# Preparing weights beside the attention and parking them off the chip in a fused attention, gMLP and mixer kernel

## The chip, the cores and the metric

The kernel runs on one NeuronCore of one Trainium2 chip. The metric is the device time of one launch in microseconds, the median of three runs. The profile is of one execution, taken by the hardware profiler. TensorE is called PE, VectorE DVE, ScalarE ACT, GpSimd POOL; SP is the engine whose queue issues nearly all DMAs.

## The reference

```python
q_pool = q.reshape(4, 8, 576, 2, 64).mean(axis=3)
attn = softmax(q_pool @ k.T / 8)          # 576 x 1152 for each of 4*8 heads
x = heads_side_by_side(attn @ v)          # 4 x 576 x 512
h = gelu(x @ w_in)                        # w_in 512 x 1024
u, v = h[..., :512], h[..., 512:]
v_n = layernorm(v) * g_ln
v_s = einsum('ts,bsd->btd', w_sg, v_n) + b_sg[:, None]   # w_sg 576 x 576
x = x + (u * v_s) @ w_out                 # the gating block, w_out 512 x 512
x = x + (relu(x.T @ w_tok1) @ w_tok2).T   # token mixing, 576 -> 256 -> 576
out = x + relu(x @ w_ch1) @ w_ch2         # channel mixing, 512 -> 1536 -> 512
```

All inputs but `w_sg`, `g_ln`, `b_sg`, `q`, `k`, `v` arrive as float64 and have to be turned into float32 on the chip.

## The kernel before, in words

Every product but two of the attention's is made in three passes: a float32 is split in a high part (a float32r copy) and a low part (what the copy lost), and PE multiplies high by high, high by low and low by high (`products`, line 186). So each weight block has two tiles, high and low (`block`, line 179).

**A conversion** (`convert`, line 216) turns one 128 x 512 piece of a float64 weight into these two tiles. A DMA brings the 64-bit words into `ws` (512 KB, two buffers). ACT works out which numbers are in range (`wd`, lines 230 and 231). DVE builds the float32 in `wz` in four operations (lines 239, 243, 247 and 252). POOL copies it to the high tile (line 210) and subtracts to get the low one (line 214). `Feed` keeps a list of pieces: `add` appends and starts loads, `ops(1)` issues one of the four steps, and `until(n)` issues what is missing so that n pieces are done. The table `HOOKS` says at which points of the program a step is issued: "c" is one step of a conversion, "n" one of the layer norm, "x" one split of x, "t" and "s" the preparation of `w_sg`, "f" one of three closing steps of the attention. A name such as `2U1e` means batch 2, phase U, block 1, at its end; the trailing letter tells the place within the block.

**Attention** (`attention`, line 329) takes 16 pairs of heads. Each pair's work is handed to a planner (`Plan`, line 57) as tasks with an engine, an estimated duration, an urgency and the buffers that it takes and gives back; `Plan.run` lists them in the order in which a simulated machine would start them, and the instructions are issued in that order. Each engine runs its own instructions in that order. For one pair: q and k are loaded, POOL adds neighbouring rows of q (line 388), PE transposes q and k (lines 400 and 432), PE makes scores (line 462) and DVE their row maxima (line 469); then PE makes the scores turned round (line 513), ACT takes the exponential (line 521), POOL adds the exponentials up in `acc` (line 527), PE multiplies by v (line 536), PE sums `acc` over partitions (line 549), DVE inverts the sum (line 560) and writes x (line 567). Scores of both kinds share three PSUM buffers. Of the weights only the first block, the half of `w_in` that makes v (four pieces), is converted here, one step of the 16 about every 26 us. Its first two loads are issued by `feed.add` ahead of the plan, so ahead of q and k.

**Gating** (`spatial`, line 717), for each batch b: V (line 807) makes v for 576 tokens in groups of 256, 256 and 64, followed by gelu on ACT and DVE (lines 707 to 714) and statistics (lines 820 and 821); O (line 915) multiplies the batch before by `w_out`; U (line 873) makes u in four blocks with gelu; S (line 891) is the product with `w_sg`, after which DVE adds the bias (line 900), POOL multiplies by u (line 903) and ACT and DVE split the result (lines 905 and 906). The layer norm (`v_norm`, line 826) runs between, in small pieces; its low parts are POOL's (line 858, shown as line 214 of the helper). V, U and S of all batches share three PSUM buffers of two banks. In batch 0 the kernel also converts the u half of `w_in` (four pieces, loaded through ACT's queue and SP's) and `w_out` (four), and prepares the gate's matrix `w_sg`: it is loaded into `gu`, split by ACT and POOL (`wsg_split`), transposed by PE in both parts and copied out by ACT (`wsg_tr`, line 764). U's block fb waits until its piece is converted, and S waits for all of `w_sg`.

**Mixing** (`mixing`, line 1034): K (line 1088) and Q (line 1098) are the two token products, with transposes of x between (line 1070). Then nine chunks of 256 tokens each take a channel product (`psc`, line 1151), transposes (`pu`, line 1163) and a second channel product (`po`, line 1171). From batch 3's U on, 30 pieces are converted here: 12 of `w_ch1`, 6 of the token weights, and 12 of `w_ch2`, the last ones in the first chunk, between its products.

## Time and profile before

| | |
|---|---|
| median of 3 runs | 1238.43 us (1237.66 to 1239.03) |
| the profiled execution | 1238.36 us, of which the span from first to last instruction is 1236.5 us |
| busy PE, DVE, ACT, POOL | 94%, 58%, 37%, 49% of the span |
| mean granted clock of PE | 0.978 of full speed |

Full speed of PE's clock is 2.4 GHz and its other level 1.2 GHz, so a granted clock of 0.81 over a stretch is a mix of the two. A busy share says little by itself: PE shows 94% busy and still the time goes up and down with the stretches in which it isn't. The stages have to be read one by one: attention to about 564 us, gating from there to about 832 us, token mixing to 910 us, channel mixing to the end.

### The profile page before, as it was taken

Reading aid. Unit: us, or ns where it says so; the run is one execution under the profiler, and the core shown is the slowest. Engines: PE = TensorE matmul, PEld = TensorE weight load, DVE = VectorE, ACT = ScalarE, POOL = GpSimd, SP = SyncE. Lnnn points to the kernel's source line nnn. Section 1 sums busy time; section 2 is a strip of 40 time slices with the busy share of each in tenths; the row PEclk is TensorE's granted clock in tenths of the full one; section 3 lists DMA queues with packets and bytes.
Section 4 is the critical chain, followed back from the end, with each engine's and each line's share of the span. In section 5 each row is a group of like instructions: output and inputs, shape, how many; then the busy total and the mean of one; then the engine's idle time right before and its main releaser. Section 6 shows DMA issues by size and latency. Waiting matters only on the chain.

```text
span 1236.5 us, 22054 instructions
## 1 busy us (share of the span) xinstructions
PE 1162.6 (94%) x9269; PEld 949.0 (77%) x9269; DVE 711.1 (58%) x1017; ACT 458.5 (37%) x847; POOL 611.5 (49%) x452
## 2 busy tenths in 40 slices
PE   3899999999999999998579999979989999999998
PEld 2577777777767777765569898968877899999887
DVE  4767767776676666643976464799987112121111
ACT  1244454445444444453552423434433111111111
POOL 1477877877777777786473414263365111100100
PEclk9899999999999999998789999989998999999999
DMA  6412222222122211002220000023232000000000
GB/s 149 94 40 59 59 56 58 59 59 59 44 55 59 52 46 39 21 1 77 69 62 17 1 1 1 18 69 111 88 100 86 10 17 10 17 18 18 18 17 18
DMA packets 63332, 57.32 MB, mean 46 GB/s; under 512 B 39936, under 2 KB 51968, under 8 KB 63232
## 3 DMA queue, kind: packets, MB, share of 16 engines
q1 hardware_dynamic: 62176, 54.85, 16.3%
q8 instruction: 73, 1.20, 0.4%
q10 hardware_dynamic: 1056, 1.05, 0.3%
q14 instruction: 27, 0.22, 0.1%
HBM read 51.17 MB, written 4.72 MB: 45 GB/s over the span
## 4 chain that ended last, share of the span: by engine, by line
PE 37%; DVE 10%; ACT 1%; issue 1%; POOL 1%; DVEq 0%; ACTq 0%; POOLq 0%
PE psc L1151 11%; PE po L1171 11%; PE pss L891 5%; PE psv L807 3%; DVE wz L247 2%; PE psu L873 2%; PE psz L915 2%; DVE wz L243 2%; DVE wz L252 1%; DVE wz L239 1%; DVE y L214 1%; PE pso L915 1%; PE pu L1163 1%; DVE xT L1102 1%; PE psh L1098 0%
## 5 line engine op out<-in xcount | busy, mean ns | idle before, releaser
L527 POOL TENSOR_TENSOR acc<-acc,e 128x576 f32<-128x576 f32 x224 | 319.7, 1427 | 83.6 <-ACT e L521 65.2
L469 DVE TENSOR_REDUCE mx<-s 128x2 f32<-128x768 f32 (+1 forms) x240 | 225.8, 950 | 115.1 <-PE s L462 111.9
L521 ACT ACTIVATE e<-sT 128x576 f32<-128x576 f32 x288 | 184.2, 652 | 180.0 <-PE sT L513 172.9
L462 PE MATMUL s<-k,q 64*128 64x384 f32 (+1 forms) x1440 | 178.7, 351 | 2.5 <-DVE mx L469 1.9
L513 PE MATMUL sT<-q,k 64*128 64x288 f32 x1728 | 177.3, 307 | 2.6 <-DVE mx L469 1.9
L513 PEld LDWEIGHTS sT<-q,k 64*128 64x128 f32 x1728 | 135.4, 185 | 44.3 <-issue 34.5
L536 PE MATMUL po<-e,vn 128*64 128x288 f32 x1152 | 160.1, 413 | 0.0
L1151 PEld LDWEIGHTS psc<-x,w 128*128 128x128 f32 x1296 | 156.8, 190 | 3.3 <-DVE gc L1078 2.5
L1151 PE MATMUL psc<-x,w 128*128 128x256 f32 x1296 | 157.1, 283 | 2.3 <-DVE gc L1078 2.3
L1171 PE MATMUL po<-w,gc 128*128 128x512 f32 x648 | 156.4, 401 | 2.3 <-POOL w L214 1.7
L1171 PEld LDWEIGHTS po<-w,gc 128*128 128x128 f32 x648 | 121.8, 189 | 32.9 <-POOL w L214 2.5
L462 PEld LDWEIGHTS s<-k,q 64*128 64x128 f32 (+1 forms) x1440 | 116.3, 178 | 19.0 <-issue 10.3
L1077 ACT ACTIVATE gc<-psc 128x256 fp32r<-128x256 f32 x108 | 41.0, 384 | 229.9 <-PE psc L1151 229.9
L536 PEld LDWEIGHTS po<-e,vn 128*64 128x64 f32 x1152 | 75.3, 136 | 60.8 <-issue 20.1
L1078 DVE SCALAR_TENSOR_TENSOR gc<-psc,gc 128x256 fp32r<-128x256 f32 x108 | 45.5, 424 | 100.2 <-ACT gc L1077 100.2
L210 POOL TENSOR_SCALAR x<-xT 128x1024 fp32r<-128x1024 f32 x9 | 9.6, 1069 | 173.6 <-PE psc L1151 173.2
L1178 DVE TENSOR_TENSOR ob<-po,us 128x512 f32<-128x512 f32 x18 | 12.4, 691 | 133.5 <-PE po L1171 133.5
L513 PE MATMUL sT<-nmT,pick 64*128 64x288 f32 x576 | 88.2, 290 | 0.0
L560 DVE RECIPROCAL den<-den 128x288 f32<-128x288 f32 x32 | 62.3, 1947 | 35.6 <-ACT den L556 35.6
L891 PE MATMUL pss<-wsg,vn 128*128 128x288 f32 x448 | 74.6, 315 | 1.8 <-POOL vn L214 1.8
L891 PEld LDWEIGHTS pss<-wsg,vn 128*128 128x128 f32 x448 | 63.9, 193 | 12.0 <-issue 5.4
L873 PE MATMUL psu<-x,w 128*128 128x288 f32 x384 | 56.0, 307 | 10.1 <-issue 8.6
(117 smaller groups left out, 1519.0 us busy)
## 6 DMA issues: line engine op xcount, KB each, us to landing
ws<-in_moe_w_ch_dram SPq DMA_DIRECT2D x24, 512.0 KB, 3.5
qn<-in_q_dram SPq DMA_DIRECT2D x32, 288.0 KB, 4.4
kn<-in_k_dram SPq DMA_DIRECT2D x32, 288.0 KB, 4.1
vn<-in_v_dram SPq DMA_DIRECT2D x32, 288.0 KB, 3.2
out_dram<-ob SPq DMA_DIRECT2D x18, 256.0 KB, 2.0
ws<-in_moe_w_in_dram SPq DMA_DIRECT2D x6, 512.0 KB, 4.7
ws<-in_moe_w_out_dram SPq DMA_DIRECT2D x4, 512.0 KB, 3.5
gu<-in_moe_w_sg_dram SPq DMA_DIRECT2D x1, 1152.0 KB, 5.8
```

The lines of the kernel that those rows point to most:

```text
L462: nc.tensor.matmul(ps[0:m, h, 0:KC], flat(c.q[x])[r, t * P:t * P + m], c.k[y][r, cs], start=(n == 0), stop=(n == 2))
L469: nc.vector.tensor_reduce(out=mx[i % 2][0:m, t, :, g], in_=ps[0:m, :, 0:KC], axis=AX.X, op=ALU.max, negate=True)
L513: nc.tensor.matmul(ps[:, h, 0:TC], left, right, start=(n == 0), stop=(n == 3))
L521: nc.scalar.activation(out=s.e[j], in_=ps[:, :, 0:TC], func=AF.Exp)
L527: eng.tensor_tensor(out=s.acc, in0=s.e[0] if j == 1 else s.acc, in1=s.e[j], op=ALU.add)
L536: nc.tensor.matmul(s.po[D * h:D * h + D, 0:TC], c.vn[:, h, j], s.e[j][:, h], start=(j == 0), stop=(j == J - 1))
L560: nc.vector.reciprocal(out=s.den, in_=s.den)
L873: nc.tensor.matmul(ps[:, ch, 0:TC], wiu[sw][:, cc, fb * P:(fb + 1) * P], X[sx][:, cc, ch * TC:(ch + 1) * TC], start=first, stop=end)
L891: nc.tensor.matmul(ps[:, ch, 0:TC], V[sx][r, ti, db * P:(db + 1) * P], L.ws[sw][r, ti, ch * TC:(ch + 1) * TC], start=first, stop=end)
L1078: nc.vector.scalar_tensor_tensor(out=l_, in0=ps, scalar=0.0, in1=f32(h_), op0=ALU.max, op1=ALU.subtract)
L1151: nc.tensor.matmul(ps, WC1[f // 4][sw][:, cc, (f % 4) * P:(f % 4 + 1) * P], u[sx][:, cc], start=first, stop=end)
L1171: nc.tensor.matmul(pos[tt], g[sx][:, f, tt * P:(tt + 1) * P], WC2[f // 4][sw][:, f % 4], start=(f == 0 and n == 0), stop=(f == NF - 1 and ...
```

## The change

- Conversions become objects (`Piece`) with a destination tile or one off the chip. The high part is now a copy by ACT; before it was a copy by POOL.
- Within the attention the planner now also places the four pieces of the v half of `w_in`, the four of the u half, the preparation of `w_sg` (five row blocks; transposed in float32 by PE, then split by ACT and DVE) and the four of `w_out`, one about every 25 us from 60 us of the plan's time. All but the first four are stored in DRAM by SP's queue from the place of their own source buffer, and fetched back at the start of the gating.
- No load of a weight goes ahead of the first loads of q and k: each waits for a marked score task.
- The twelve pieces of `w_ch2` are converted in batches 1 and 2 of the gating, one step in the middle and one at the end of each block, stored in DRAM, and fetched when mixing starts. The steps in the channel products' first chunk are gone. The pieces of `w_ch1` and of the token weights stay where they were.
- The last third of the last product with v, the last sums and x's last half pair are kept out of the plan and issued among batch 0's V products. Batch 0's splits of x go from POOL to DVE.
- The bias loads and POOL's scaling of them move from the end of batch 0's U to just after V's second group of products.
- The planner looks at 300 tasks, before at 90; the two loads of a pair's q, k or v are one task.

```diff
+    def halves(x):
+        x = x.bitcast(F32R)
+        return [x[:, s * 512:(s + 1) * 512] for s in range(2)]
...
+        def high(self):
+            if self.dst:
+                self.parts = self.dst()
+                for x in self.parts[2:]:
+                    g_scale(x, self.z, 1.0)
+            else:
+                self.parts = [self.cut(x) for x in halves(self.s)]
+            nc.scalar.copy(self.parts[0], self.z)
+        def low_part(self):
+            sub(nc.gpsimd, self.parts[1], self.z, f32(self.parts[0]))
+        def send(self, s):
+            nc.sync.dma_start(out=self.away[s], in_=f32(self.parts[s]))
...
+    def fetch(to, x):
+        for s in range(2):
+            nc.sync.dma_start(out=f32(to[s]), in_=x[s])
...
-        for n in range(4 * CC):
-            plan.add("DVE", 0.75, lambda: feed.ops(1), urgency=20.0 + 26.0 * n)
-        feed.add(*row_block(0, w_in[:, DH:2 * DH], 0))
+        def conversion(x, u):
+            a = plan.add("SP", 0.05, lambda: x.load(nc.sync), after=[mark(u)], urgency=u - 20,
+                         take=["ws"], land=4.0)
+            d1 = plan.add("DVE", 1.2, x.step1, after=[a], urgency=u, take=["wz"])
+            e = plan.add("ACT", 1.4, x.early, after=[a], urgency=u, take=["wd"])
+            d2 = plan.add("DVE", 1.3, x.step2, after=[d1], urgency=u + 0.5)
+            d3 = plan.add("DVE", 1.3, x.step3, after=[d2], urgency=u + 1)
+            d4 = plan.add("DVE", 1.3, x.step4, after=[d3, e], urgency=u + 1.5,
+                          give=[("wd", e)] + ([] if x.away else [("ws", a)]))
+            h = plan.add("ACT", 0.65, x.high, after=[d4], urgency=u + 2)
+            l_ = plan.add("POOL", 1.4, x.low_part, after=[h], urgency=u + 2, give=[("wz", d1)])
+            if x.away:
+                for s in range(2):
+                    plan.add("SP", 0.05, lambda s=s: x.send(s), after=[h, l_][s:s + 1],
+                             urgency=u + 3 + s, land=3.5, give=[("ws", a)])
...
+        todo = [w0_piece(j) for j in range(CC)] + col_pieces(A.w1, w_in, 0)
+        todo += list(range(NTT)) + col_pieces(A.wo, w_out, 0)
+        for n, x in enumerate(todo):
+            u = 60.0 + 25.0 * n
+            if isinstance(x, int):
+                gate_weights(x, u)
+            else:
+                conversion(x, u)
+        for n in range(3):
+            feed.add(*row_pieces(A.c2[n], w_ch2, 512 * n))
...
         def finish():
-            yield lambda: None
-            yield lambda: None
+            yield lambda: [f() for f in rest[:-2]]
+            yield lambda: [f() for f in rest[-2:]]
             yield lambda: a2.close()
...
+            if name[0] in "12" and name[-1] in "mz":
+                feed.ops(1)
...
         def open_up(close):
             close()
             open_left()
-            splits.extend([lambda ti=ti: wsg_split(ti) for ti in range(CC)])
-            pieces.extend([lambda ti=ti, s=s: piece(ti, s) for ti in (CC, *range(CC))
-                           for s in range(2 if ti < CC else 1)])
-            L.io = feed.add(*col_block(2, w_out, 0))
+            for s in range(2):
+                nc.sync.dma_start(out=f32(L.ws[s][:, 0:CC]), in_=A.ws[s][:, 0:CC])
+                for r in range(0, P, TAIL):
+                    nc.sync.dma_start(
+                        out=f32(L.ws[s][r:r + TAIL, CC:NTT]), in_=A.ws[s][0:TAIL, CC:NTT])
+            fetch(L.wo, A.wo)
+            bias_load()
...
-        wsg_load()
+        fetch(W[1], A.w1)
...
+        fetch(W[4], A.c2[0])
...
-            feed.add(*row_block(i, w_ch2, 512 * (i - 4)))
+            fetch(W[i], A.c2[i - 4])
...
-                    feed.until(io + f + 1)
-                    hook(f"N{f}")
```

In the new `HOOKS` batch 0 has "f" after V's first products (`0V0a`), at the end of V's first group (`0V0z`) and after V's second products (`0V1a`); "x" for x's splits at `0V0m` (two), `0V1m`, `0V2a` and `0V2e`; and no "c". The "c" entries from batch 3's U to `Q31` and `M10` are as before.

## Rows read from the trace of the kernel before

**Rows 1.** Busy time by stretch: attention, batch 0, batches 1 and 2, then S3 to Q3.
```profile
core 0: us, PE busy (x) PEld busy (x) DVE busy (x) ACT busy (x) POOL busy (x), PEclk, DMA share, GB/s
52.00:564.00 512.00, 509.35 (x5186) 370.10 (x5184) 341.72 (x435) 249.82 (x455) 396.98 (x271) 1.00 0.19 47
564.00:653.00 89.00, 62.40 (x338) 52.56 (x335) 64.06 (x85) 41.97 (x82) 55.15 (x46) 0.81 0.25 78
...
653.00:764.00 111.00, 111.00 (x712) 101.35 (x710) 58.57 (x103) 36.33 (x56) 39.90 (x33) 1.00 0.00 1
...
801.00:911.00 110.00, 99.04 (x602) 85.31 (x601) 104.80 (x140) 46.56 (x76) 52.49 (x48) 0.97 0.29 89
```

**Rows 2.** PE in order of time, 563 to 633 us: start, duration, instruction, [idle before].
```profile
563.25 3.13 PE L536 MATMUL po<-e,vn 128*64 128x288 f32 x24
571.05 1.23 PE L549 MATMUL pt<-acc,ones 128*64 128x288 f32 x4 [4.67 <-POOL acc L527]
...
598.77 5.30 PE L873 MATMUL psu<-x,w 128*128 128x288 f32 x24 [8.59 <-issue]
...
633.01 19.92 PE L891 MATMUL pss<-wsg,vn 128*128 128x288 f32 x112
```

**Rows 3.** PE in order of time, 902 to 953 us.
```profile
904.58 6.01 PE L1098 MATMUL psh<-x,r 128*128 128x288 f32 x43 [0.99 <-DVE r L1078]
910.42 8.71 PE L1151 MATMUL psc<-x,w 128*128 128x256 f32 x72
...
953.10 17.99 PE L1151 MATMUL psc<-x,w 128*128 128x256 f32 x144
```

**Rows 4.** SP's queue at the start, and PE's first work.
```profile
0.73 0.86 SPq L221 DMA_DIRECT2D ws<-in_moe_w_in_dram  x2
...
5.35 0.60 SPq L379 DMA_DIRECT2D kn<-in_k_dram  x1
...
15.48 1.09 PE L432 MATMUL pt<-ident,kn 128*128 128x128 f32 x4 [15.48 <-DMA kn<-in_k_dram]
```

**Rows 5.** Attention: transposes among PE's other work; DVE, POOL and PE around 93 us.
```profile
365.33 0.66 PE L432 MATMUL pt<-ident,kn 128*128 128x128 f32 x4
...
92.74 3.15 DVE L243 SCALAR_TENSOR_TENSOR wz<-ws,wz 128x512 int32<-128x512 int32 x1
...
92.68 2.65 POOL L388 TENSOR_TENSOR qs<-qn 64x1152 f32<-64x1152 f32 x1 [1.17 <-PE pt L400]
...
96.81 0.67 PE L513 MATMUL sT<-q,k 64*128 64x288 f32 x6 [0.99 <-DVE mx L469]
```

**Rows 6.** What writes `wz`, 60 to 560 us (3 pieces): busy DVE and POOL.
```profile
60.00:560.00 500.00, 15.53 (x12) 5.71 (x6) 1.00 0.19 47
```

**Rows 7.** The chain that ended last, batch 2: V, U and S without a stall.
```profile
707.57 13.99 PE psv L807 x60
...
734.27 12.72 PE psu L873 x96
746.99 17.93 PE pss L891 x112
```

**Rows 8.** DVE and ACT behind batch 0's first V group, in order of time.
```profile
572.86 1.95 DVE L560 RECIPROCAL den<-den 128x288 f32<-128x288 f32 x1 [7.42 <-ACT den L556]
574.85 1.65 DVE L567 TENSOR_TENSOR xT<-os,den 128x288 f32<-128x288 f32 x1
582.88 1.22 DVE L708 SCALAR_TENSOR_TENSOR sq<-sq,psv 128x1024 f32<-128x1024 f32 x1 [6.38 <-ACT sq L707]
...
586.77 0.69 DVE L820 BATCH_NORM_STATS2 lst<-gv 128x6 f32<-128x512 f32 x1
...
584.35 1.06 ACT L713 ACTIVATE sq<-sq 128x1024 f32<-128x1024 f32 x1 [1.51 <-DVE sq L708]
```

**Rows 9.** POOL before batch 0's S: the low parts of the layer norm.
```profile
628.82 4.63 POOL L214 TENSOR_TENSOR vn<-gv,vn 128x512 fp32r<-128x512 f32 x3 [1.78 <-ACT vn L857]
```

**Rows 10.** The page's DMA issues: KB each, us to landing.
```profile
gu<-in_moe_w_sg_dram SPq DMA_DIRECT2D x1, 1152.0 KB, 5.8
```

**Rows 11.** What writes `wz`, 801 to 953 us (28.75 pieces): busy DVE and POOL.
```profile
801.00:953.00 152.00, 99.23 (x115) 59.07 (x59) 0.96 0.29 89
```

**Rows 12.** POOL between S3's last two gate products.
```profile
824.05 0.98 POOL L210 TENSOR_SCALAR x<-wz 128x512 fp32r<-128x512 f32 x1 [1.50 <-DVE wz L252]
```

**Rows 13.** The chain that ended last: two later channel chunks.
```profile
988.77 17.20 PE psc L1151 x144
1005.96 0.87 PE pu L1163 x8
1006.84 16.80 PE po L1171 x72
```

More of the change, by code (lines that the diff above doesn't have):

```diff
@@ L67, in ring, with add @@
         self.rings[name] = (n, [])
-    def add(self, eng, dur, fn=None, after=(), urgency=0.0, take=(), give=(), land=0.0):
+    def add(self, eng, dur, fn=None, after=(), urgency=0.0, take=(), give=(), land=0.0,
+            late=False):
         t = dict(eng=eng, dur=dur, fn=fn, after=[x for x in after if x], urgency=urgency,
-                 take=list(take), last=[], land=land, end=None, n=len(self.tasks))
+                 take=list(take), last=[], land=land, late=late, end=None, n=len(self.tasks))
         for ring, owner in give:
@@ L182, with far @@
     W = [block(wvp, "w0")]
+    away = ctx.enter_context(tc.tile_pool(name="away", bufs=1, space=bass.MemoryType.DRAM))
+    def far(name, shape):
+        return [away.tile(shape, F32, name=f"{name}{s}") for s in range(2)]
     PASSES = ((0, 0), (0, 1), (1, 0))
@@ new lines, with __init__, cut, load @@
+    class Piece:
+        def __init__(self, src, dst=None, away=None):
+            self.src, self.dst, self.away = src, dst, away
+            self.r, self.a, self.n = src.shape
+        def cut(self, x):
+            return x[:self.r, 0:self.a * self.n].rearrange("p (a n) -> p a n", a=self.a)
+        def load(self, eng):
+            s = cvp.tile([P, 512], I64, tag="ws", name="ws")
+            eng.dma_start(out=self.cut(s), in_=self.src)
+            self.s = s
+            w = s.bitcast(I32).rearrange("p (c t) -> p c t", t=2)
+            self.top, self.low = (self.cut(w[:, :, j]) for j in (1, 0))
+        def early(self):
+            self.d = d = self.cut(cvp.tile([P, 512], F16, tag="wd", name="wd", bufs=1))
+            nc.scalar.activation(out=d, in_=self.top, func=AF.Abs, scale=2.0 ** -20)
+            nc.scalar.activation(out=d, in_=d, func=AF.Abs, bias=m1024[:self.r])
+        def step1(self):
+            self.z = self.cut(cvp.tile([P, 512], F32, tag="wz", name="wz"))
@@ L276, in load, with steps @@
             while self.todo and len(self.ready) + (self.live is not None) < 2:
-                self.ready.append(convert(*self.todo.pop(0)))
-        def early(self):
-            self.cur[0]()
+                self.ready.append(self.todo.pop(0))
+                self.ready[-1].load(nc.sync)
+        def steps(self, x):
+            x.step1()
+            x.early()
+            yield
+            x.step2()
+            yield
+            x.step3()
+            yield
+            x.step4()
+            x.high()
+            x.low_part()
+            if x.away:
+                for s in range(2):
+                    x.send(s)
         def ops(self, n):
@@ L661, in tasks @@
                 po = None
+                last = i == NPAIR - 1 and x == 1
                 for js in ((0, 1, 2), (3, 4, 5), (6, 7, 8)):
@@ L666, in tasks @@
                                   take=["po"] if po is None else [],
+                                  late=last and js[-1] == J - 1,
                                   give=[("e", es[j]) for j in js] +
@@ L679, in tasks @@
-                r_ = plan.add("DVE", 2.0, lambda x=x: over(i, x), after=[d_], urgency=at + 8)
+                              urgency=at, take=["den"], give=[("tr", s_)], late=last)
+                r_ = plan.add("DVE", 2.0, lambda x=x: over(i, x), after=[d_], urgency=at + 8,
+                              late=last)
                 plan.add("DVE", 0.5, lambda x=x: x_out(i, x), after=[r_, o_], urgency=at + 9,
-                         give=[("os", o_), ("den", d_)])
+                         give=[("os", o_), ("den", d_)], late=last)
@@ new lines, in attention @@
+        for n, x in enumerate(todo):
[6 more added lines that the diff above has]
+            feed.add(*row_pieces(A.c2[n], w_ch2, 512 * n))
+        early = []
+        rest = []
+        order = plan.run()
+        for n, t in enumerate(order):
+            if n == len(order) - 40:
+                for ti in range(len(EARLY_ON)):
+                    early.append(x_early(ti))
+            if t["late"]:
+                rest.append(t["fn"])
+            elif t["fn"]:
@@ L925, in wo_act @@
             yield
-        splits, pieces, lns, xs_ = [], [], [], []
+        lns, xs_ = [], []
         def hook(name):
@@ L1147, in mixing @@
             for f in range(NF):
[L1148 removed]
+                feed.until(count[f] if i == 0 else 0)
                 ps = pc1.tile([P, 512], F32, tag="c1", name="psc1")[:, 0:NB]
```

218 lines of the change are left out of this document (96 added, 122 removed), and 40 rows, old and new, of the table HOOKS.

## Prediction

> **What bounds the kernel now.** I read busy time by stretch first, then PE in order of time where PE is not full, then the chain that ended last. In the attention PE is busy 509.35 of 512 us, in batches 1 and 2 of the gating 111 of 111 [rows 1]: PE sets the pace there, and the other engines have room (DVE 342 of 512 and 59 of 111). Three places leave PE waiting. At the start it does nothing until 15.48 us, when k lands [rows 4]. In batch 0, 564 to 653 us, it is busy 62 of 89 us at a granted clock of 0.81 [rows 1]; a whole batch without a stall is V 13.99 + U 12.72 + S 17.93 = 44.6 us, O left out, since batch 0 has none [rows 7]. From 801 us DVE is busy 104.8 of 110 us with conversions [rows 1], and the first channel chunk takes 953.10 - 910.42 = 42.7 us where a later one takes 17.20 + 0.87 + 16.80 = 34.9 us [rows 3, 13]. The change works on all three and pays with work put where PE is full.
>
> **The start.** Before k's second half, eight DMAs are queued: 2 of 512 KB (`ws`), then six of 288 KB, kn's second being the issue at 5.35 us [rows 4]. That is 2752 KB, landed at 15.48 us. Now only four of 288 KB (qn, kn) come first. If time goes by bytes, 1152 of 2752 KB of the 14.75 us since the first issue gives 6.2 us, a gain of 8.6 us; if only the 1024 KB of `ws` are saved, it is 5.5 us. I take **-7** (ends -8.6 and -5.5), and it reaches the end because PE is full from 52 to 564 us.
>
> **The attention's added work.** PE gets 25 transposes for `w_sg`. Four transposes among other PE work take 0.66 us, four alone 1.09 us [rows 5, 4]: 4.1 to 6.8 us, nothing hides them. I take **+4**, since they stand among other work. DVE gets eight more conversions at 15.53/3 = 5.2 us [rows 6] and ten subtractions, about 48 us on 342 of 512; POOL and ACT get some 10 and 25 us on 397 and 250. This is hidden unless it makes a row maximum late. It can: at 92.74 us a step lasted 3.15 us beside a POOL addition from 92.68 to 95.33 us, and PE then waited 0.99 us for a row maximum [rows 5]. The three converted pieces in this stretch hold two such losses, 0.65 us each piece, so eight more pieces cost about 5 us; the planner now knows these steps and puts row maxima first, so I take **+4** (ends 0 and 10). SP's stores and loads stand in one queue with q, k and v: a late store delays a load, but each pair's loads are asked for most of a 32 us period ahead.
> The Trainium skill (SBUF — State Buffer, "Who interferes with whom") says that a DVE instruction with two SBUF inputs and a GpSimd instruction that reads SBUF exclude each other for a whole instruction. The 3.15 us agree with it. By it alone, nothing would be added to the sum, as long as DVE's idle third takes the waits; it feeds the slower rival below.
>
> **The handover and batch 0.** The last scores end about 563.3 us, and now 563.25 us starts only half of the 24 last products with v (3.13 us) [rows 2]; V's first group follows at 564.8. Its 24 products are 13.99/60 = 0.233 us each [rows 7]: to 570.4. Then the other half of the v products to 572.0, and the sums, whose `acc` is ready at 571.05 [rows 2], so the 4.67 us of waiting are gone: to 572.7. V's second group runs to 578.3. What is late next is **DVE**: the sum's copy and V's square on ACT to 574.3, then front 1.22, tanh 1.06, back about 1.22, statistics two times 0.69 with a small aggregate each, reciprocal 1.95, x's last pair (at most 1.65, the row beside a busy POOL), to about 582.5 [rows 8]; only then the split of the tail of x, to 583.2, so V's third group of 12 products ends at 586.0; the second group's gelu and statistics take DVE to 588.5, and x's first two splits and the third group's front, 0.7 us each, to 590.6. So U starts at 590.6, not 598.77 [rows 2]. U no longer waits for conversions: 12.72 us and about 1.3 for a lowered clock after two idle stretches of 5 us, to 604.6. Then the last gelu and the layer norm's last low parts on POOL, three for 4.63 us [rows 9]: S in effect starts at 610.2 and ends at 629, against 633.01 + 19.92 = 652.9 [rows 2]. That is **-24**.
> The fetched weights: `gu` brought 1152 KB in 5.8 us [rows 10]; at that pace the u block (2 MB) lands ten us after attention's end, before U. The second `w_sg` tile, `w_out` and the bias wait for memory that x's last pair frees at 582.5: 3.8 MB, an estimate of 19 us, to 602. POOL's scaling of the bias stands in POOL's queue ahead of all low parts, so it is the one new wait that counts; at 602 us it only just clears. Ends: PE alone, 564.8 + 14 + 2.3 + 12.7 + 17.9 = 612, so -41; with POOL free 10 us later, -14.
>
> **Batches 1 and 2.** 48 steps, 12 pieces, spread over 58 places. A piece costs DVE 99.23/28.75 = 3.5 us at the end of the kernel and 5.2 in the attention [rows 11, 6]: 42 us on 58.6 of 111, so 91% busy, with the 5.2 end 109%. In 801 to 911 us, at 95%, PE lost 10% of its time [rows 1], part of it by waits that have nothing to do with DVE. Two `ws` buffers now come back only after a store; store and next load are some 9 us of a cycle of 8 to 10, so a step may wait for its load with gelu queued behind it on DVE, and PE's three buffers are the cover. I take **+5** (ends 0 and 14).
>
> **Mixing.** S3 to K2 keep their conversions. The high part leaves POOL: its 0.98 us stand between the last two gate products [rows 12], so **-1** (ends -3 and +4, the latter for 2 MB of `w_ch2` fetched in front of the pieces' loads). From Q2 on no steps are left: the first chunk becomes like the later ones, 42.7 - 34.9 = 7.8, and the 0.99 us wait in Q3 goes [rows 3]: **-9** (ends -10 and -4). The other 4 MB have 24 us until the second channel product needs them.
>
> **The sum.** -7 + 4 + 4 - 24 + 5 - 1 - 9 = -28. Against the profiled execution, 1238.36 us (the median is 1238.43, the same), that is 1210.4, so 1210.
>
> **The rivals.** (a) The forecast, 1200 to 1220: chance 0.46. (b) DVE's chain in the handover is covered by PE's buffers, nothing in the attention or batches 1 and 2 is late: -41, 0 and 0 instead of -24, +4 and +5, so 1184, about 1190 with half of it: 0.19. For it speaks that PE was never held up long in the attention [rows 1]; against it the DVE chain counted above. (c) The way back from DRAM is late: POOL stands at the bias, low parts and S wait, -14 or worse, 1220 to 1226: 0.14. For it speaks the one SP queue with 5 MB; against it `gu`'s pace. (d) DVE becomes the bound of batches 1 and 2, +14 and more for slower gates, 1219 to 1228: 0.13. (e) **Slower**: conversions in the attention come as four steps in a row beside POOL's additions, each 3 us as at 92.74, and three score buffers are used up by the first of them. To pay for everything else (-32 without the disturbance) twelve pieces would have to hold PE 2.7 us each, four times the 0.65 us seen; at 4 us each it is +48 - 32, 1254. Chance 0.06: DVE idles a third of the attention, but in pieces. (f) The change doesn't do what it says: S still waits for the parked `w_sg` as long as for its preparation, and the mixing's gain is eaten in (d): about 1236, 0.02.
>
> **How the numbers follow.** Likeliest is (a), 1210. Leaving out half of (b), all of (e) and (f) and a little at each edge, the range is 1191 to 1228. A measurement of this kernel tells 0.2%, 2.5 us, from no change. Faster by more than that holds (a) to (d) and parts of the rest: 0.93; within it 0.02; slower 0.05.
>
> **What would show it.** PE's first transposes near 8 us; attention's end near 564, as the start's gain pays for the added work; V's first product without a gap behind the attention, U at about 590 and S's end near 629; DVE about 90% busy in batches 1 and 2 with PE idle 5 us; a first chunk of 35 us with no `wz` in it. I am wrong if row maxima hold PE for over 10 us in the attention, if POOL's scaling of the bias ends after 605, or if PE idles over 14 us in batches 1 and 2.

## The result, and the profile of the changed kernel

| | before | changed |
|---|---|---|
| device time, median | 1238.05 us | 1255.35 us (1254.34 to 1257.3) |
| ratio | | 1.0145, 95% [1.0125, 1.0166] |
| profiled execution: its time, its span | 1238.36, 1236.5 us | 1255.77, 1253.2 us |

The kernel became **slower by 17 us** where I had predicted 28 us less. I cut both traces at the same events on PE and set each difference beside the term of the sum that it answers to ("psc" is the first product of the channel mixing):

| stretch | before | changed | difference | predicted |
|---|---|---|---|---|
| span's start to first transpose of k | 15.48 | 8.67 | -6.8 | -7 |
| to the end of the last scores | 547.8 | 558.6 | +10.8 | +8 |
| to V of batch 1 | 89.5 | 68.7 | -20.8 | -24 |
| **V of batch 1 to V of batch 3** | 112.0 | 147.1 | **+35.1** | **+5** |
| **to the first psc** | 145.7 | 152.5 | **+6.8** | **-1** |
| the first chunk | 42.7 | 34.9 | -7.8 | -9 |
| the rest | 283.4 | 282.8 | -0.6 | 0 |

Four terms were near, two were not, and those two make the sign. The stretches of the changed kernel by busy time, columns as in [rows 1]: attention, handover and batch 0, batches 1 and 2, to the first psc, first chunk.

```profile
8.67:567.30 558.63, 541.24 (x5391) 392.44 (x5393) 429.64 (x521) 276.51 (x509) 421.66 (x278) 0.99 0.30 75
567.30:636.02 68.72, 56.52 (x296) 46.75 (x297) 36.01 (x57) 21.08 (x35) 24.65 (x20) 0.85 0.35 124
636.02:783.10 147.08, 121.97 (x718) 108.38 (x717) 93.61 (x148) 57.51 (x91) 54.41 (x43) 0.94 0.26 86
783.10:935.57 152.47, 137.86 (x835) 120.58 (x833) 113.30 (x170) 63.43 (x107) 44.77 (x34) 0.96 0.20 65
935.57:970.44 34.87, 34.87 (x227) 31.57 (x226) 6.29 (x14) 5.68 (x14) 6.90 (x4) 1.00 0.31 121
```

The third row is the case. PE was full there before [rows 1]; now it is busy 121.97 of 147.08 us. 25.1 us are idle, and another 10.0 are the same products at a lower granted clock (0.94 on the mean, a mix of the two levels). DVE, the engine that got the work, is busy 93.61 us: 64%, not the 91% I had worked out, and still PE waits. For whom, in that stretch (us in all, times, longest):

```profile
PE psz L1016 <- DVE gv L844: 7.2, 3, 3.5
PE psu L974 <- DVE xT L1025: 6.5, 6, 1.9
PE pss L992 <- POOL vn L216: 6.2, 2, 4.8
PE psu L974 <- DVE gu L844: 3.0, 2, 2.4
PE pss L992 <- DVE gu L844: 2.2, 2, 1.4
```

18.9 of the 25.1 us end on DVE (the last step of a gelu, `gv` and `gu`, and the residual `xT`), 6.2 on POOL's low parts of the layer norm.

**The handover** went by the prediction's steps in the main. PE in order of time:

```profile
574.49 1.68 PE L574 MATMUL po<-e,vn 128*64 128x288 f32 x12
...
...
587.38 1.20 PE L908 MATMUL psv<-w,x 128*128 128x512 f32 x4 [2.39 <-DVE x L216]
591.11 2.29 PE L974 MATMUL psu<-x,w 128*128 128x288 f32 x8 [2.52 <-ACT x L355]
...
616.15 20.04 PE L992 MATMUL pss<-wsg,vn 128*128 128x288 f32 x104 [1.83 <-POOL vn L216]
```

The other half of the v products stands between V's groups, and V's third group waits for DVE's split of x. That U starts at 591.11, where 590.6 was predicted, is luck: the last scores end at 567.3 and not at 563.3, so U starts 23.8 us behind them and not 27.3. What follows is longer than I had it. U takes 17.1 us instead of 14.0, at a granted clock of 0.77. S starts in earnest at 616.15, 48.9 us behind the scores instead of 46.9, after waits for the layer norm's parts on ACT and POOL, and runs 20.04 us instead of 18.8, at 0.83. Together that is the -20.8 for -24.

**Batches 1 and 2.** Here is the longest stall, one of the two that end on POOL, where U gives way to S in batch 1, all engines in order of time; `ws` and `wz` are the piece, `vn` and `sq` the gating.

```profile
679.68 0.60 ACT L958 CAST vn<-gv 128x512 fp32r<-128x512 f32 x1
...
680.36 1.28 POOL L216 TENSOR_TENSOR vn<-gv,vn 128x512 fp32r<-128x512 f32 x1 [3.57 <-ACT vn L958]
680.48 1.70 DVE L267 SCALAR_TENSOR_TENSOR wz<-wd,wz 128x512 f32<-128x512 f16 x1
...
682.26 0.62 ACT L277 CAST ws<-wz 128x512 fp32r<-128x512 f32 x1 [1.98 <-POOL vn L216]
682.79 0.65 ACT L243 ACTIVATE wd<-ws 128x512 f16<-128x512 int32 x1
...
682.96 1.27 POOL L216 TENSOR_TENSOR ws<-wz,ws 128x512 fp32r<-128x512 f32 x1 [1.32 <-ACT ws L277]
683.47 0.72 ACT L244 ACTIVATE wd<-wd,m 128x512 f16<-128x512 f16 x1
684.10 0.63 ACT L837 ACTIVATE sq<-psu 128x576 f32<-128x576 f32 x1
684.75 0.61 ACT L958 CAST vn<-gv 64x512 fp32r<-64x512 f32 x1
...
685.51 1.26 POOL L216 TENSOR_TENSOR vn<-gv,vn 64x512 fp32r<-64x512 f32 x1 [1.28 <-ACT vn L958]
...
686.83 3.60 PE L992 MATMUL pss<-wsg,vn 128*128 128x288 f32 x11 [4.83 <-POOL vn L216]
```

ACT copies V's last but one tile at 679.68 and the last, 64 rows whose input was normalized with batch 0, at 684.75. Between the two, in ACT's queue, stand the copy of a piece's high part, which starts 0.08 us after the piece's fourth step ends on DVE (680.48 + 1.70), the next piece's test (two instructions) and a gelu's square. POOL's low part of the piece goes first there too. Only at 685.51 POOL makes V's last low part, and PE has waited 4.83 us. A step of a piece is cheap on each engine; what costs here is its place in three queues at once. The Trainium skill (PSUM — Partial Sum Buffer, "Engine vs sequencer instructions") calls the queues of these three engines strict FIFO; the trace agrees: the copy of a tile normalized a batch ago comes 4.5 us after the end of the copy before it (684.75 - 680.28).

ACT's waits for the fourth step, before its copies of high parts, V of batch 1 to V of batch 3:

```profile
ACT ws L277 <- DVE wz L267: 27.5, 9, 5.1
```

### The profile page after: what moved, and what is told of

The parts are those of the page before. It is cut to its first block, busy times and chain, and to the rows that moved or that the text cites. A ratio compares the mean times of both kernels' runs of the same rounds, so it can differ in the third digit from the quotient of the medians.

```text
span 1253.2 us, 22164 instructions
## 1 busy us (share of the span) xinstructions
PE 1171.5 (93%) x9249; PEld 952.1 (76%) x9249; DVE 734.6 (59%) x1032; ACT 471.2 (38%) x868; POOL 574.9 (46%) x398
## 4 chain that ended last, share of the span: by engine, by line
PE 32%; DVE 7%; issue 6%; POOL 2%; ACT 2%; DMA 1%; POOLq 0%; DVEq 0%; ACTq 0%; SPq 0%
PE psc L1238 12%; PE po L1258 12%; PE pss L992 3%; DVE wz L261 1%; DVE wz L255 1%; PE psh L1185 1%; POOL vn L216 1%; PE psv L908 1%; DVE wz L267 1%; PE psz L1016 1%; DVE y L216 1%; PE pu L1250 1%; PE psr L1175 1%; POOL gt L1004 1%; DVE g L216 1%
## 5 line engine op out<-in xcount | busy, mean ns | idle before, releaser
L565 POOL TENSOR_TENSOR acc<-acc,e 128x576 f32<-128x576 f32 x224 | 328.5, 1466 | 62.4 <-ACT e L559 43.7
L1238 PEld LDWEIGHTS psc<-x,w 128*128 128x128 f32 x1296 | 155.9, 189 | 0.7
L1258 PE MATMUL po<-w,gc 128*128 128x512 f32 x648 | 153.3, 396 | 0.0
L992 PE MATMUL pss<-wsg,vn 128*128 128x288 f32 x448 | 82.3, 334 | 17.1 <-POOL vn L216 10.9
L1265 DVE TENSOR_TENSOR ob<-po,us 128x512 f32<-128x512 f32 x18 | 12.5, 692 | 145.7 <-PE po L1258 145.7
L992 PEld LDWEIGHTS pss<-wsg,vn 128*128 128x128 f32 x448 | 69.4, 208 | 29.8 <-POOL vn L216 11.9
L598 DVE RECIPROCAL den<-den 128x288 f32<-128x288 f32 x32 | 62.3, 1946 | 19.3 <-ACT den L594 19.3
L974 PE MATMUL psu<-x,w 128*128 128x288 f32 x384 | 59.5, 318 | 13.0 <-DVE xT L1025 6.5
```

Source lines behind the costliest of these rows:

```text
L565: eng.tensor_tensor(out=s.acc, in0=s.e[0] if j == 1 else s.acc, in1=s.e[j], op=ALU.add)
L598: nc.vector.reciprocal(out=s.den, in_=s.den)
L974: nc.tensor.matmul(ps[:, ch, 0:TC], wiu[sw][:, cc, fb * P:(fb + 1) * P], X[sx][:, cc, ch * TC:(ch + 1) * TC], start=first, stop=end)
L992: nc.tensor.matmul(ps[:, ch, 0:TC], V[sx][r, ti, db * P:(db + 1) * P], L.ws[sw][r, ti, ch * TC:(ch + 1) * TC], start=first, stop=end)
L1238: nc.tensor.matmul(ps, WC1[f // 4][sw][:, cc, (f % 4) * P:(f % 4 + 1) * P], u[sx][:, cc], start=first, stop=end)
L1258: nc.tensor.matmul(pos[tt], g[sx][:, f, tt * P:(tt + 1) * P], WC2[f // 4][sw][:, f % 4], start=(f == 0 and n == 0), stop=(f == NF - 1 and ...
```

## The experiments

Two theories to begin with. **Q**: ACT's copy of the high part is issued behind the fourth step, and holds ACT's queue (27.5 us above) with gelu behind it. **N**: a step costs about its own time on DVE wherever it stands. Two more, L and M, came later. All times below are us; "1 to 3" is V of batch 1 to V of batch 3, "3 to psc" what follows.

| run | 1 to 3 | 3 to psc | first chunk | median | ratio, 95% |
|---|---|---|---|---|---|
| changed | 147.1 | 152.5 | 34.9 | 1255.35 | 1.0145 |
| e1_highpool | 143.6 | 145.5 | 34.9 | 1246.82 | 1.0069 [1.0054, 1.0084] |
| e2_defer | 146.4 | 152.2 | 34.9 | 1250.96 | 1.0100 [1.0083, 1.0117] |
| e3_late | 112.0 | 155.9 | 43.3 | 1231.99 | 0.9949 [0.9934, 0.9964] |
| e4_late_pool | 112.0 | 146.0 | 42.2 | 1222.63 | 0.9875 [0.9859, 0.9891] |
| e5_su | 127.9 | 157.3 | 34.9 | 1240.11 | 1.0013 [1.0003, 1.0022] |
| e6_vo | 144.4 | 144.9 | 34.9 | 1245.86 | 1.0055 [1.0039, 1.0071] |
| e9_dveonly | 129.8 | 147.5 | 42.3 | 1239.86 | 1.0019 [1.0007, 1.0031] |
| e10_rest | 118.6 | 146.2 | 42.5 | 1227.51 | 0.9922 [0.9907, 0.9937] |
| e11_dvehalf | 117.8 | 146.4 | 42.2 | 1226.61 | 0.9913 [0.9898, 0.9928] |
| e13_early | 139.6 | 146.5 | 34.9 | 1241.16 | 1.0025 [1.0014, 1.0036] |
| e14_gpool | 125.8 | 148.9 | 42.9 | 1237.25 | 0.9996 [0.9987, 1.0006] |
| e15_four | 116.0 | 147.1 | 38.9 | 1219.28 | 0.9856 [0.9838, 0.9873] |
| e16_four_early | 116.1 | 147.2 | 38.9 | 1222.31 | 0.9874 [0.9859, 0.9888] |
| e17_four_s | 112.0 | 150.6 | 37.4 | 1220.06 | 0.9862 [0.9846, 0.9879] |
| e18_four_u | 123.0 | 147.5 | 37.4 | 1227.91 | 0.9914 [0.9900, 0.9929] |

### The copy of the high part

e1_highpool: the changed kernel with that copy, behind the attention, on POOL, as before the change.

```diff
-            x.high()
+            x.high(lambda o, i: g_scale(o, i, 1.0))
```

> The changed kernel, but the high part of every piece that is converted after the attention is copied by POOL again instead of ACT. Theory Q (queues): batches 1 and 2 lost 35 us because ACT's copy stands in ACT's queue waiting for DVE's fourth step while the gelus behind it wait; without the copy on ACT batches 1 and 2 fall from 147 to 115-128 us and the whole to 1222-1236. Rival D (DVE's work): the twelve pieces' own DVE time in batches 1 and 2 is what costs; then they stay at 142-150 us and the whole stays within 1248-1258.

e2_defer: the copy, the low part and the stores are issued where the next step stands; the rest of the edit lets the next piece begin there.

```diff
             x.step4()
+            yield
             x.high()
...
```

> The changed kernel, but a piece's copy by ACT, its subtraction by POOL and its stores are issued at the next step's place instead of right behind DVE's fourth step, so that ACT and POOL find the step done. Same work on the same engines. Theory Q: batches 1 and 2 fall to 115-128 us, the whole to 1222-1236. Rival D: no change, 1248-1258. Rival S (the store's way back: two source buffers that come free only after a store): slightly longer, since stores go out later, 1255-1262.

Measured: e1 takes 7.0 us off "3 to psc", all of the excess there, and only 3.5 of the 35.1. So Q is the second failed term and a tenth of the first. POOL has to wait for the fourth step too (37.2 us before its copies in batches 1 and 2), so e1 compares the two queues; what a copy without any wait would give is not shown. e2 takes off 0.7 and 0.3, but it hardly removed the wait that it was made to remove. ACT in batches 1 and 2 of e2:

```profile
ACT ws L277 <- DVE wz L267: 26.6, 8, 5.1
```

The fourth step is mostly still not done at the next step's place, so e2 is no test of Q. How the copy does harm between batch 3 and the mixing shows in the waits; the changed kernel:

```profile
ACT w L277 <- DVE wz L267: 32.1, 12, 5.5
...
PE pso L1016 <- ACT g L1006: 7.9, 2, 4.4
...
PE psh L1185 <- ACT r L1164: 2.7, 4, 1.0
```

and e1_highpool:

```profile
PE pso L1016 <- ACT g L1006: 6.0, 2, 4.8
...
PE psh L1185 <- ACT r L1164: 0.4, 1, 0.4
```

ACT stands 32.1 us before copies whose fourth step isn't done, and the gate and the mixing's relu come late by 4.2 us in these two waits alone. With the copy on POOL, PE waits for POOL no longer than before (2.1 us in that stretch, 2.9 in the changed kernel). PE's idle time there falls by 5.3 us, from 14.6 to 9.3; in the other 1.7 of the 7.0 its products are shorter (busy 136.2 us, not 137.9). The length of ACT's wait alone tells little: in the kernel before, ACT stands 30.2 us in this stretch for fourth steps, ahead of its tests, and PE's waits for the gate and the relu are those of e1.

### The 48 steps taken out

e3_late converts `w_ch2` late as the kernel before does, and keeps the rest of the change; e4_late_pool is e3 with e1's edit.

```diff
-        for n in range(3):
-            feed.add(*row_pieces(A.c2[n], w_ch2, 512 * n))
...
-            if name[0] in "12" and name[-1] in "mz":
-                feed.ops(1)
...
-            fetch(W[i], A.c2[i - 4])
+            feed.add(*row_block(i, w_ch2, 512 * (i - 4)))
```

> The changed kernel, but the twelve pieces of the last matrix are converted where they were before, among mixing and the first channel products, not in batches 1 and 2, and not parked; ACT still copies. All theories: batches 1 and 2 go back to 112 us (-35), the first channel chunk back to about 43 us (+8), so 1225-1229. If batches 1 and 2 stay over 120 us, something else of the change slows them.

> As the run before, and the copy of the high part is POOL's again after the attention. Theory Q says that the stretch from batch 3's V to the first channel product (145.5 us before, 152.5 after) falls back to 144-147, so the whole is 5-8 us under the run before. Rival: that stretch grew for another reason (the fetch of 2 MB in front of the pieces' loads); then it is back already in the run before, and this one equals it within 2 us.

Measured: 112.0 us in both, the time of before to 0.1 us: the +35.1 is the 48 steps, with their loads, tests, copies and stores, and nothing else. The first chunk goes back to 42 to 43 us. e4 beats both kernels, by 1.25% [1.09, 1.41] against the kernel before.

### The steps in other places

e5_su and e6_vo are e1 with the steps at the places of U and S, or of V and O (e6: `name[1] in "VO"`, every place). L in their expectations says that DVE is full in V and O and has room in S; N is as above. (A letter holds for its own group of runs: the L further down is another theory.)

```diff
-            if name[0] in "12" and name[-1] in "mz":
+            if name[0] in "12" and name[1] in "US" and name[-1] in "mez":
```

> As the run with POOL's copy after the attention (first run, batches 1 and 2 took 143.6 us), but the 48 steps of batches 1 and 2 stand in U and S alone, three to a block, none in V and O. Theory L (DVE is full locally: in V and O it already worked without a pause before, in S it idled more than half): batches 1 and 2 fall to 115-128 us, the whole to 1217-1231. Rival N (each step costs PE its own 0.7 us of DVE wherever it stands): 140-150 us, the whole 1243-1253. Rival S (source buffers come back only after a store, so bunched steps wait for their loads): over 147 us, with DVE waiting for the DMA of ws by far more than 2.6 us.

> As the run before, but the steps stand in V and O alone (four to a block, 52 places). Theory L: worse than the 143.6 us of even spreading, 150 us or more, the whole 1253 or more. Rival N: 140-150 us, as everywhere. Rival S: over 147 us, by waits for loads.

Measured, over V of batch 1 to psc: 285.1 and 289.3 us, e1 289.1, e4 258.0. e5's 127.9 in batches 1 and 2 is where L had it, but its "3 to psc" is 11.8 us longer than e1's. In each the stall only moves: e5 loses it in V of the next batch, most of it waiting for x's split on ACT and POOL, e6 before U, waiting for DVE's residual (20.7 us). 27 to 31 us for 48 steps, some 0.6 us a step: that spoke for N.

### What of a step costs

Three kernels add to e4 what nobody reads, at the 48 places: the DVE instructions alone (e9_dveonly), all the others with loads and stores (e10_rest), and the DVE instructions at half the length (e11_dvehalf). `Only` is a piece whose `load`, `early`, `high` and `low_part` do nothing, with 512 or 256 columns; `Rest` one whose four steps do nothing.

```diff
+        feed2.add(*[Only() for _ in range(12)])
...
+            if name[0] in "12" and name[-1] in "mz":
+                feed2.ops(1)
```

> e4_late_pool with 48 steps put into batches 1 and 2 at the same 48 places, but only their DVE instructions: four per piece, of the same kinds and sizes, on data that a memset made once. No loads, no instructions on ACT or POOL, no stores, and nobody reads what they write; the result of the kernel is that of e4_late_pool. Theory N (a step costs about its own time on DVE, because batches 1 and 2 hang on chains that go through DVE, in order): V1 to V3 112.0 -> 135 to 147, span 1242 to 1252. Rival X (what costs is what hangs on the steps: ACT's two and POOL's two instructions, loads and stores in the queues): V1 to V3 at most 122, span at most 1229.

> e4_late_pool with everything of the 12 pieces in batches 1 and 2 but their DVE instructions: 12 loads, 24 ACT instructions for the test of the exponent, 12 ACT copies, 12 POOL subtractions (from a tile that a memset made once), 24 stores whose data nobody fetches. Theory N: V1 to V3 112.0 -> 112 to 117, span 1218 to 1224. Rival X: 127 to 147, span 1234 to 1253.

> e9_dveonly with each of the 48 instructions on 256 columns in place of 512. Theory N with no slack: a bit over half of what e9_dveonly adds, +13 to +18 in V1 to V3. Rival S (DVE has slack, and only what goes beyond it costs): +6 or less. Rival C (it is the number of instructions and their places in the order, not their length): as e9_dveonly within 4.

Batches 1 and 2 by busy time, in the order e4, e9, e10, e11 (columns as in [rows 1]):

```profile
635.51:747.50 111.99, 111.99 (x718) 102.17 (x717) 58.43 (x101) 35.77 (x55) 37.31 (x31) 1.00 0.00 1
```
```profile
635.36:765.12 129.76, 119.06 (x718) 106.73 (x717) 95.41 (x149) 35.12 (x55) 40.93 (x33) 0.96 0.02 5
```
```profile
635.50:754.05 118.55, 114.46 (x719) 103.59 (x717) 59.38 (x101) 57.04 (x91) 52.85 (x44) 0.99 0.31 107
```
```profile
635.09:752.92 117.83, 113.78 (x719) 102.45 (x717) 83.57 (x148) 35.13 (x55) 39.55 (x33) 1.00 0.02 5
```

DVE's part alone costs 17.8 us, everything else 6.6. e10 keeps the pieces' copies on ACT, so the whole that belongs to these parts is the changed kernel's 35.1: 10.7 more than the parts. (e1, with the copies on POOL, loses 31.6.) N, with 23 to 35 for e9, falls, and so does X (what hangs on the steps) by both; of e11's three, S (here: slack) fits. At half length DVE gets 25.1 us more work for 5.8 us, at full length 37.0 for 17.8: 25.1 - 5.8 = 19.3 and 37.0 - 17.8 = 19.2 us are free at these places, and from one run to the other each us more costs one. Not all of that is waiting: in e9 PE idles 10.7 us, and the other 7.1 are its products at the granted clock of 0.96. So DVE has room, but some 19 us and not the 54 in which it isn't busy.

I took the missing 34 for DVE's waits in its own order (**L**): 18.3 us for ACT's copy of the gate, 11.3 for tanh. Two runs tested that. e14_gpool moves the gate's low part, and so that wait, from DVE to POOL in e9; e13_early is e1 with ACT's test beside the third step instead of the first.

```diff
-            sub(nc.vector, two(L.g[1][:, db]), g, two(f32(L.g[0][:, db])))
+            sub(nc.gpsimd, two(L.g[1][:, db]), g, two(f32(L.g[0][:, db])))
```
```diff
             x.step1()
-            x.early()
...
             x.step3()
+            x.early()
```

> e9_dveonly (its 48 DVE instructions stay) with the subtraction that makes the low part of the gate on POOL instead of DVE, so that DVE no longer stands waiting for ACT's copy of the gate (20.1 us of waits in batches 1 and 2). Theory L (a wait in DVE's order costs like work): V1 to V3 129.8 -> 112 to 119. If DVE's busy time alone counts: 124 to 127, the subtractions' own time. If POOL's queue becomes what S and the low parts wait for: 127 or more.

> e1_highpool, with ACT's two instructions for the test of the exponent issued with a parked piece's third step instead of its first, when the load has long landed and the last piece's fourth step is past. Theory L with ACT's part in it: V1 to V3 143.6 -> 130 to 137, span 1242.5 -> 1229 to 1236, ACT's waits for the load and for the fourth step (18.0 and 15.4 us) mostly gone. If ACT's place in the queue doesn't matter: 141 to 146, span 1240 to 1245.

e14 came out at 125.8, where L had 112 to 119 and DVE's busy time alone 124 to 127: L falls. PE's waits in it, 8.2 us for the layer norm's low parts, the residual and U's gelu, are in e9 too, each to 0.1 us; e9 has one more, 2.4 us for V's gelu. With the handoff gone DVE just waits for PE in S instead (10.9 us, 0.6 in e9): S was not where the time was lost. e13 gave back 4.0 of e1's 31.6 us, less than the 6.6 at least that was expected; ACT's waits for loads and for the fourth step fell from 33.4 to 13.9 us. So the test's place is part of the loss. What makes up the rest of the 10.7 us that the parts don't explain was not traced.

### The place

e14 sent me to DVE's load by stage in place of a mean. V, O, U and S of batch 2, in e4_late_pool and in the changed kernel:

```profile
690.15:704.14 13.99, 13.99 (x62) 11.25 (x61) 7.24 (x9) 4.01 (x5) 4.67 (x5) 1.00 0.01 2
704.14:716.85 12.71, 12.71 (x98) 12.71 (x96) 9.82 (x26) 2.58 (x4) 1.16 (x1) 1.00 0.00 1
716.85:729.57 12.72, 12.72 (x99) 12.72 (x97) 6.72 (x9) 5.38 (x10) 4.66 (x5) 1.00 0.00 0
729.57:747.50 17.93, 17.93 (x114) 15.51 (x113) 6.91 (x9) 5.28 (x9) 8.70 (x7) 1.00 0.00 1
```
```profile
705.75:719.75 14.00, 14.00 (x63) 11.25 (x62) 5.93 (x7) 6.09 (x11) 9.62 (x9) 1.00 0.27 95
719.75:742.08 22.33, 13.60 (x97) 12.75 (x95) 16.51 (x30) 7.70 (x12) 2.05 (x2) 1.00 0.25 83
742.08:762.01 19.93, 15.06 (x97) 14.20 (x97) 15.20 (x29) 9.34 (x17) 8.10 (x7) 0.91 0.38 131
762.01:783.10 21.09, 19.73 (x112) 16.87 (x113) 10.34 (x12) 6.15 (x12) 11.85 (x9) 0.92 0.26 76
```

O and U take 25.4 us, and DVE is busy 16.5 of them without any step: layer norm, residuals and gelus come together there. The steps in O and U of the changed kernel (DVE's busy time on `wz`, count, granted clock, DMA):

```profile
719.75:742.08 22.33, 4.80 (x8) 1.00 0.25 83
742.08:762.01 19.93, 7.03 (x9) 0.91 0.38 131
```

These 17 steps take 11.8 us. 16.5 + 11.8 = 28.3, more than the 25.4 us hold, by 2.9. O and U of batch 2 grew by 16.8 us, V by nothing, S by 3.2. In V and S there is room (14.2 busy of 31.9). Hence **M**: the place decides, not the number. e15_four parks a third of `w_ch2` alone (16 steps, every third place), e16_four_early is e15 with e13's edit, and e17_four_s and e18_four_u put those 16 steps at the 16 places of S, or of U.

e15, on e4:

```diff
+        feed.add(*row_pieces(A.c2[2], w_ch2, 1024))
...
+                if len(places) % 3 == 1:
+                    feed.ops(1)
```

e17, on e15 (e18 with "U"):

```diff
-                if len(places) % 3 == 1:
+            if name[0] in "12" and name[1] == "S" and name[-1] in "mz":
```

> e4_late_pool with four pieces (the last third of w_ch2, 16 steps, every third of the 48 places) parked in batches 1 and 2, the other eight converted late. Theory L: 16 steps are some 13 us of DVE, under the 20 that are spare, so V1 to V3 112.0 -> 113 to 118, with a first chunk 42.2 -> 38 to 41: total 1219 to 1226 against 1222.6. If every step costs its own time: V1 to V3 122 to 126, total 1227 to 1233.

> e15_four with ACT's test issued with the third step for the four parked pieces. Theory L with ACT's part in it: V1 to V3 1 to 4 us less than in e15_four. If ACT's place in the queue doesn't matter: the same within 1.

> e15_four with its 16 steps at the 16 places of S in batches 1 and 2, one at each. Theory M: DVE in S 6.3 -> 13 of 18 us, so nothing is late: V1 to V3 112 to 113.5 (e15_four: 115.95), span 1216 to 1218.5, total about 2 to 3 us under e15_four. If a step costs wherever it stands (handoffs of S, gates late for the next batch's products): 115 or more.

> e15_four with its 16 steps at the 16 places of U in batches 1 and 2, one at each. Theory M: DVE in O and U 16.8 -> 23 of 25.4 us, with bunches in U (6.7 -> 13 of 12.7): V1 to V3 117 to 124, 4 to 10 us more than e17_four_s. If it is the number of steps, not the place: equal to e17_four_s within 2.

In batches 1 and 2 the same 16 steps cost 0.0 us in S, 4.0 spread out, 11.0 in U. M holds for the place. Its reason was only half right: in e18 O and U themselves are on time (12.7 us each) and S begins late. e18 where U ends, in order of time:

```profile
669.79 0.60 ACT L962 CAST vn<-gv 128x512 fp32r<-128x512 f32 x1
...
671.35 0.68 ACT L244 ACTIVATE wd<-ws 128x512 f16<-128x512 int32 x1 [0.96 <-ACT vn L962]
671.36 0.73 POOL L213 TENSOR_SCALAR ws<-wz 128x512 fp32r<-128x512 f32 x1 [4.59 <-DVE wz L268]
...
672.17 1.29 POOL L217 TENSOR_TENSOR ws<-wz,ws 128x512 fp32r<-128x512 f32 x1
...
673.35 0.61 ACT L962 CAST vn<-gv 64x512 fp32r<-64x512 f32 x1
...
673.41 2.62 POOL L217 TENSOR_TENSOR vn<-gv,vn 128x512 fp32r<-128x512 f32 x2
...
676.09 14.19 PE L996 MATMUL pss<-wsg,vn 128*128 128x288 f32 x76 [2.79 <-POOL vn L217]
```

V's copy is done at 670.4, but POOL waits 4.59 us for the piece's fourth step and then makes the piece's two parts before it comes to V's low parts at 673.41; ACT's test stands before the last copy. The layer norm's chain through DVE, ACT and POOL ends where S begins, and a piece put there lengthens it on every engine. In e17 the same happens once at the other end, on x's split for V of batch 3:

```profile
756.78 0.62 POOL L213 TENSOR_SCALAR ws<-wz 128x512 fp32r<-128x512 f32 x1 [2.25 <-ACT sq L841]
757.48 1.27 POOL L217 TENSOR_TENSOR ws<-wz,ws 128x512 fp32r<-128x512 f32 x1
...
760.12 2.07 PE L912 MATMUL psv<-w,x 128*128 128x512 f32 x4 [2.18 <-POOL x L217]
```

After it "3 to psc" takes 150.6 us, 4.6 more than in e4: PE idles 2.2 us more, and its products take 2.3 more at a granted clock of 0.95 (e4: 0.98). From V of batch 1 to psc the 16 steps so cost 4.6 us in S, 5.1 spread out and 12.5 in U: S is far better than U, but hardly better than spreading. The total, 1220.06, is no better than e15's 1219.28 either, so the 2 to 3 us that were expected are not shown. (The profiles are no measure of it: e15's is of an execution of 1222.36 us, its longest.) e16 shows no gain over e15. e4, e15 and e17 all beat both kernels, the one before by 1.25 to 1.44%; their intervals overlap, and which is best is open.

### The start and the attention

e7_nogate is e4 without the preparation of `w_sg` (`todo` without its five tiles): no transposes, splits and stores, and other bytes are fetched in its place. e8_start and e12_start2 are the kernel before with the start of the change: in e8 the planner issues the first weight loads, in e12 also each pair of loads of q, k and v is one task.

```diff
-        feed.add(*row_block(0, w_in[:, DH:2 * DH], 0))
+        feed.add(*row_block(0, w_in[:, DH:2 * DH], 0), load=False)
+        plan.add("SP", 0.05, feed.load, urgency=-20.0)
```

and in e12

```diff
-                first = plan.add("SP", 0.05, lambda: f(i, 0, *a), urgency=u, take=[ring], land=3.5)
...
+                return [plan.add("SP", 1.0, lambda: (f(i, 0, *a), f(i, 1, *a)), urgency=u,
+                                 take=[ring], land=4.0)]
```

> As the run with the last matrix late and POOL's copy (1222.6 us), but the preparation of w_sg in the attention is left out (25 transposes by PE, their splits and stores), and as many bytes are fetched in its place, so the sums of the gate are not the reference's. The attention took 558.5 us from its first transpose to its last scores, 547.8 before. If the gate's transposes and splits are a good half of the 10.8 us, it falls to 551-553 and the whole to 1215-1218. If the eight more conversions are what costs (row maxima late), it stays at 556-558 and the whole at 1220-1223.

> The kernel before, but the first two loads of weights are issued behind the first loads of q, k and v instead of ahead of them. My term of the start: PE's first work at 8.5 us instead of 15.5, the whole 1231-1232 (-6.8). If the gain is lost later in the attention (PE waiting for the second pair's loads or for row maxima), 1235-1238.

> The kernel before with the two halves of each load of q, k and v as one task of the planner, and the first loads of weights issued by the planner behind the first q and k. That is the start of the change without the rest of it. If the start's gain is the queue's: PE's first transpose 15.48 -> 8.5 to 9.5, last scores 563.3 -> 556.5, total -6 to -7. If a faster start is lost again in the attention (row maxima, other loads late): first transpose 9, last scores over 560, total above -3.

e7: the attention takes 556.5 us, e4 558.3, total 1221.22 against 1222.63: the gate's preparation costs about 2 us. e8 didn't make the edit that was meant: the planner put both weight loads behind q's first half, PE began at 15.11, and the time is that of before. In e12 they came once more between q and k. SP's queue, e12 and the changed kernel:

```profile
1.98 1.05 SPq L221 DMA_DIRECT2D ws<-in_moe_w_in_dram  x2
3.08 2.44 SPq L380 DMA_DIRECT2D kn<-in_k_dram  x2
```
```profile
2.00 2.10 SPq L417 DMA_DIRECT2D kn<-in_k_dram  x2
```

PE begins at 12.00 us in e12, the last scores end at 559.4 (563.3 before), and the span is 4.3 us shorter; the ratio is 0.9982 [0.9972, 0.9992], which is 2.2 us [1.0, 3.5]. So 3.5 us at the start reach the end of the attention and, within that interval, the kernel's. The 1024 KB of weights in front of k are worth 12.00 - 8.67 = 3.3 us, and the 576 KB of v that stood before k's second half 15.48 - 12.00 = 3.5: the gain is the queue's, but it doesn't go by bytes at one pace.

## Why the prediction was wrong

**Batches 1 and 2 (+5, ends 0 and 14; measured +35.1): the failed step.** It read "42 us on 58.6 of 111, so 91% busy", then took the loss from a stretch where PE lost 10% with DVE at 95% [rows 1]. The work itself was near: 38.5 us for the 48 steps, 42 forecast. Wrong was dividing it by the mean of two batches. DVE is busy 16.5 of 25.4 us in O and U of batch 2 and 14.2 of 31.9 in V and S; at the change's places 19 us were free and the rest paid in full (e9, e11), and the same 16 steps cost 0 or 11 us there by place (e17, e18). Nor was DVE the only queue: ACT's test and copy and POOL's subtraction were costed at nothing, the load was named without a price, and all of these cost 6.6 us alone and 10.7 more together with DVE's part (e10). And 10.0 of the 35.1 us are products at a lower granted clock, beside the 25.1 of idle time. The clock's share I had counted for batch 0 (1.3 us in U; its products took 16.2 us instead of 12.72, at 0.77), and not here. Rival (d) named the stage and the engine, at +14 "and more"; it was short of the rest.

The Trainium skill (Perfetto Trace Analysis, "Identifying the Most-Contended Engine") goes by occupancy for DVE, ACT and POOL. By it DVE, at 64% in batches 1 and 2 of the changed kernel, has a third to spare; the runs differ, since 18.9 of PE's 25.1 idle us there end on DVE, and taking DVE's steps away alone leaves 6.6 of the 35.1 us (e10), and the measurement decides.

**Mixing (-1, ends -3 and +4; measured +6.8): the other failed step.** "The high part leaves POOL" counted what POOL gains and not whose queue takes the copy, with a wait for DVE's fourth step in front of it. e1 against the changed kernel and e4 against e3 show 7.0 and 9.9 us for that.

**Attention (+8, measured +10.8).** PE is busy 6.1 us more (541.24 against 535.15) and idle 4.7 more. The 25 transposes, forecast at 4, take 4.50 us, though e7 makes the gate's own share only 2 when the planner orders the rest anew. The disturbed row maxima, also at 4, fit the idle time only by luck. PE's waits for them in the changed kernel are this one and 1.3 us more:

```profile
PE s L500 <- DVE mx L507: 2.8, 7, 0.8
```

That is 4.1 us in all, and 3.8 in the kernel before. What grew are PE's waits for DVE's copies of the transposed q and k (7.9 us, before 5.1) and for what DVE does after the maxima (`nm`, 1.5, before none): DVE is late, but not with the maxima. Rival (e), the slower one, put its loss here and was wrong: it was 11 us, not 48.

**Start, handover, first chunk** (-7, -24, -9) came at -6.8, -20.8 and -7.8. The start's working by bytes was wrong: the 1024 KB of weights were worth 3.3 us and not 5.5 (e12), and the rest is v's place in the queue. The handover had two errors against each other, as said above. The first chunk gained just what its own products had to gain; the 0.99 us wait in Q3, counted there, gave way to 2.7 us of waits for ACT's relu. Rival (c), the way back from DRAM, did not come about: POOL's scaling of the bias is over at 600.3. Of the signs I had named, "PE idles over 14 us in batches 1 and 2" is the one that occurred.

## What to carry to other kernels

Room for moved work is to be read by stage, and in each engine's queue at the place where the work is put: ask what stands behind it there, and who waits for that, down to PE. A step that is cheap on three engines lengthens a chain that crosses all three, and one that waits for another engine brings that engine's delay into its own queue. Before parking much of it, try a few steps where no chain ends, and measure as far as the next stage: here 16 steps in U cost 11 us on the spot, and in S nothing on the spot but 4.6 us in the stage behind.

## What the chip showed that I had not expected

- A DVE step of 0.68 us takes 1.70 us when it begins beside a POOL instruction of 1.28 us (680.36 and 680.48 above); the 48 steps take 38.5 us where 12 times the medians of their four kinds (0.42, 0.68, 0.69, 0.68) are 29.7. The Trainium skill (SBUF — State Buffer, "Who interferes with whom") has two-input DVE instructions and reading POOL instructions exclude each other, and the trace agrees. The gating's own POOL work is enough for that: in e9, where the pieces have none, the steps take 41.8 us. In the changed kernel all ten of the 48 steps that took over 0.9 us ran beside a POOL instruction; three of the ten are the step with one input (up to 1.52 us).
- The way through DRAM was short. The page gives 2.3 us for a store of 256 KB to DRAM and 7.3 us for a fetch of 1024 KB, and DVE waited 2.6 us in all for loads in batches 1 and 2.
